# Routing of tokens with fewer VectorE operations, and the second item's expert and rows made first

## The chip, the cores and the metric

The kernel runs on one core of one Trainium2 chip. The metric is the device time of one execution in microseconds (us), the median of several runs. Engines are named as in the profile: PE is TensorE, DVE is VectorE, ACT is ScalarE, POOL is GpSimd, SP is SyncE, which issues most DMAs.

## What is computed

Three stages follow each other: attention, a mixture of experts with one expert for each token (MoE), and a dense layer (moe2).

```python
def attn(q, k, v):                       # 4 batches, 8 heads, 576 tokens, 64
    scores = where(causal window of 128, q @ k.T / 8 - slope[h] * |i - j|, -1e9)
    return softmax(scores) @ v           # 2304 tokens x 512

def moe(x, modality_id, w_gate, modality_bias, w1, w2):    # 8 experts
    logits = x @ w_gate + modality_bias[modality_id]
    e_idx = argmax(logits, axis=1)
    gate_w = softmax(logits)[arange(N), e_idx]
    out[tokens of e] = gate_w * (relu(x @ w1[e]) @ w2[e])  # w1 512x1024, w2 1024x512

def moe2(x, w_in, w_out):
    h = x @ w_in                         # 512 x 2048
    return (h * cos(h)) @ w_out
```

## The kernel before

**Attention** (0 to 186 us) runs over 36 units of four heads and 128 rows. The 2304 tokens are 18 blocks of 128. When a pair of blocks is done, its routing runs between the units: `logits(t)` gives `products` (the logits of 256 tokens as 16 rows: 8 experts as a high and a low part, ls), `choose` (ls transposed to tokens on partitions, parts and bias added, the largest found, ties broken by rev; the result is the one-hot oh, with a bf16 copy ohb) and `ranks(t)`: PE matmuls with the triangular matrix tri and the matrix ones count for each token how many earlier ones chose the same expert. cum is the running sum of oh over the pairs. DVE's `fold` (a multiplication and a reduction) picks the rank of the own expert, and the rank is split into rank // 128 and rank % 128 (pf). `one_hot` of the second part is ob.

**Items.** A work item is up to 256 tokens of one expert; nine items follow each other, each in eight steps (n = 0 to 71, and three more, since the second product lags by three). A step of item i has 12 matmuls `up` (xT with s1, the split of w1) and 12 matmuls `down` (hh with s2, the split of w2). Weights come in pieces of 512 KB on SP's queue (`load_w1`, `load_w2`) into r1 and r2, with two buffers each; the expert's number is read from the tile regs into a register of SP first (L230). ACT casts a piece into the high half of s, DVE subtracts it for the low half: both are needed for the product. POOL gathers an item's tokens with indirect DMAs (xg), PE transposes them and ACT and DVE split them into xT. Items 0 to 8 alternate between two tiles xT0 and xT1.

Item 0 takes its expert and rows from `early()`, which looks at the first blocks only and lets the item start before the routing is complete. All others need `late()`. Its pieces lie in the list `after`, and one is taken at each step: `sums` (for each expert the number of items, and their order), `slots` (each token's slot among the 26 blocks of 128 slots, one-hot in oa and multiplied by the row number), `table` (18 matmuls of oa with ob: the row behind each slot, idx), `experts` (the expert of each item, regs). Then `starts` and `gates`, `rows_of` and `dense`, which make the right-hand sides rhs and with 18 more matmuls the place and the gate of each token in the dense stage (tok_d, gate_d). 

**The order.** Every engine runs its instructions in the order in which they stand. Up to step 12 a scheduler sets this order by its own estimate of when things are ready; from step 12 to 66 (`InOrder`) it is the order in which the code is written. PE, DVE and ACT are each one queue. From step 10 on the conversion of the dense layer's weights (double precision words to f32, tiles mag, top, wi_a, lf) runs between the steps on DVE, ACT and POOL. The dense stage begins at about 376.

**Names.** s1_0 to s1_2 are the three split buffers of w1, s2_0 and s2_1 those of w2; numbers behind them are counted by the program. Instructions of the helpers carry the helper's line: L535 (attention and routing) and L1168 (items and dense) before, L549 and L1190 after.

Of the kernel before, what the change touches and what calls it, by code (L numbers as in the profile page):

```python
# [22 lines left out]
HALF_PI = 1.5707963267948966  # L23

# [5 lines left out]
def kernel(  # L30
# [162 lines left out]
    oh = rt.tile([128, T, NE], F32, name="oh")  # L193
    ohb = rt.tile([128, 2, NE], BF16, name="ohb")
    cum = rt.tile([128, NE], BF16, name="cum")
    iota = rt.tile([128, 128], F16, name="iota")
# [8 lines left out]
    regs = rt.tile([1, 2 * NL + 2], I32, name="regs")  # L205
    xTs = [rt.tile([128, 2, KD, SLOTS], F32R, name=f"xT{j}") for j in range(2)]
    xgs = [rt.tile([128, DM], F32, name=f"xg{j}") for j in range(2)]
    idx0 = rt.tile([128, 2], I32, name="idx0")
# [8 lines left out]
    def one_hot(out, n, at, count):  # L217
        V_.tensor_tensor(out, iota[:, 0:n].unsqueeze(1).to_broadcast([128, count, n]),
                         at.unsqueeze(2).to_broadcast([128, count, n]), op=ALU.is_equal)

    NF = FF // 128
    W1, HH = {}, {}
    E = {}
# [17 lines left out]
    def ranks(t):  # L241

        rp = E["rp"] = bank("L", [128, 3, NE])
        a, b = ohb[:, 0], ohb[:, 1]
# [6 lines left out]
        if t == 0:  # L251
            V_.tensor_tensor(cum, oh[:, 0], oh[:, 1], op=ALU.add)
# [12 lines left out]
    def early():  # L265
# [14 lines left out]
        def lacks():  # L280
# [5 lines left out]
            V_.scalar_tensor_tensor(cum[0:1], eo[0:1], short[0:1], cum[0:1], op0=ALU.mult, op1=ALU.add)  # L286
# [33 lines left out]
    def late():  # L320
# [12 lines left out]
        def sums():  # L333
            ci = rt.tile([128, 3, NE], I32, name="ci")
            V_.tensor_copy(ci[:, 2], E["rp"][:, 2])
            V_.tensor_scalar(ci[:, 0], ci[:, 2], 8, None, op0=ALU.logical_shift_right)
            V_.tensor_scalar(ci[:, 1], ci[:, 2], 255, None, op0=ALU.bitwise_and)
            V_.tensor_copy(K3[:, 0], ci[:, 0])
            V_.tensor_copy(rr, ci[:, 1])
# [14 lines left out]
            V_.tensor_scalar(A3[:, 0], pre[:, 0], 2.0, None, op0=ALU.mult)  # L354
            V_.tensor_scalar(A3[:, 1], K3[:, 0], 2.0, None, op0=ALU.mult)
            V_.tensor_tensor(endF, A3[:, 0], A3[:, 1], op=ALU.add)
            V_.tensor_tensor(A3[:, 2], pblk, endF, op=ALU.subtract)
            E["m9"] = m9

        def experts():  # L360
# [4 lines left out]
            nb = rt.tile([1, NE], F32, name="nb")  # L365
            V_.scalar_tensor_tensor(nb, K3[0:1, 1], 2.0, K3[0:1, 2], op0=ALU.mult, op1=ALU.add)
            V_.tensor_tensor(nb, nb, pblk[0:1], op=ALU.add)
            b = rt.tile(shp, F32, name="b_", tag="fold3")
            inF = rt.tile(shp, F32, name="inF")
            V_.tensor_tensor(inF, bl, rowp(A3[:, 0]), op=ALU.is_ge)  # L370
# [13 lines left out]
        def slots():  # L384
# [21 lines left out]
        def starts():  # L406
# [4 lines left out]
            n256 = rt.tile([128, 1], F32, name="n256")  # L411
            V_.tensor_scalar(n256, tot[:, 0:1], float(SLOTS), None, op0=ALU.mult)
            V_.tensor_scalar(ds, ds, n256, None, op0=ALU.add)
# [8 lines left out]
            V_.scalar_tensor_tensor(dq, A3[:, 2], 128.0, dq, op0=ALU.mult, op1=ALU.add)  # L422
# [15 lines left out]
        def rows_of():  # L438
# [3 lines left out]
            V_.scalar_tensor_tensor(dt, a3[:, 0], 128.0, dt, op0=ALU.mult, op1=ALU.add)  # L442
# [3 lines left out]
            di = rt.tile([128, T], I32, name="di")  # L446
            V_.tensor_copy(di, dt)
            dh = rt.tile([128, 2, T], I32, name="dh")
            V_.tensor_scalar(dh[:, 0], di, 7, None, op0=ALU.logical_shift_right)
# [1104 lines left out]
```

## Time and profile before

| | |
|---|---|
| median of 3 runs | 836.0 us (834.7 to 837.13) |
| the profiled execution | 837.98 us, of which the span is 836.3 |
| PE busy | 800.9 us (96%) |
| DVE busy | 615.7 us (74%) |
| ACT busy | 492.2 us (59%) |
| POOL busy | 198.3 us (24%) |

The profile is one execution. A row of a timeline gives the start, the busy time, the engine, the line, the operation with its tiles (result<-operands), shapes and count, and in brackets how long the engine was idle before it and who released it. Matmul times overlap in the pipeline, so the spacing of starts tells more about the cost of a small one than its duration does.

### The profile page before, as it was taken

The page shows a single profiled execution, that of the slowest core. Times are in us where ns is not written, and L with a number is a line of the kernel's source. Part 1 is how long each engine was busy: PE and PEld are TensorE (multiplying, and loading weights), DVE is VectorE, ACT ScalarE, POOL GpSimd, SP SyncE. Part 2 cuts the span into 40 slices and gives each one's busy share as a digit, 9 for nine tenths or more (in the row PEclk, how much of TensorE's full clock was granted, in tenths as well). Part 3 has the DMA queues.
Part 4 walks back from the last instruction along what each step waited for, and adds up shares of the span by engine and source line. Part 5 has one row for each costly group of instructions (what it writes and reads, how often), then busy time and mean ns, then how long its engine had stood idle before and what let it go on. Part 6 is the DMA issues. An engine that isn't in the chain of part 4 may idle for free. (4 is left out here: it accounts for less than half of the span.)

```text
span 836.3 us, 14761 instructions
## 1 busy us (share of the span) xinstructions
PE 800.9 (96%) x5278; PEld 704.9 (84%) x5278; DVE 615.7 (74%) x1472; ACT 492.2 (59%) x912; POOL 198.3 (24%) x256
## 2 busy tenths in 40 slices
PE   7999999998899999999999999999999999999996
PEld 5889888888889999999978788777888888888995
DVE  4767786768899999997749999886665555555562
ACT  6866766552565676665646676654544555444562
POOL 4755574411022132330001121112122002100100
PEclk9999999989899999999999999999999999999999
DMA  9664530452788888878633232402211001100000
GB/s 169 157 156 109 140 89 33 140 169 60 256 273 267 282 277 267 275 226 293 207 122 96 66 125 65 164 25 69 96 56 58 1 1 38 38 1 1 26 26 25
DMA packets 125134, 103.40 MB, mean 124 GB/s; under 512 B 61725, under 2 KB 105027, under 8 KB 125059
## 3 DMA queue, kind: packets, MB, share of 16 engines
q1 hardware_dynamic: 121043, 92.48, 37.0%
q0 software_dynamic: 2960, 9.70, 3.4%
q8 instruction: 42, 0.69, 0.3%
q10 hardware_dynamic: 1056, 0.26, 0.2%
q14 instruction: 33, 0.27, 0.1%
HBM read 85.90 MB, written 16.52 MB: 122 GB/s over the span
## 5 line engine op out<-in xcount | busy, mean ns | idle before, releaser
L1168 PE MATMUL bk<-hh,s 128*128 128x256 f32 x864 | 116.9, 283 | 5.2 <-DVE y L1168 4.5
L1168 PE MATMUL bk<-xT,s 128*128 128x256 f32 x816 | 111.8, 287 | 3.9 <-ACT s L1168 2.8
L1168 POOL TENSOR_TENSOR lf<-lf,mag 128x512 f32<-128x512 f32 x32 | 47.2, 1476 | 284.1 <-DVE mag L1168 258.9
L1168 PEld LDWEIGHTS bk<-hh,s 128*128 128x128 f32 x864 | 108.0, 189 | 6.7 <-DVE y L1168 5.3
L1168 PEld LDWEIGHTS bk<-xT,s 128*128 128x128 f32 x816 | 104.6, 195 | 4.5 <-ACT s L1168 3.0
L1168 PE MATMUL bk<-yT,wi_a 128*128 128x512 f32 (+1 forms) x480 | 104.1, 368 | 1.2 <-DVE yT L1168 0.8
L1168 PE MATMUL bk<-yT,wi_b 128*128 128x512 f32 (+1 forms) x480 | 104.8, 367 | 0.0
L1168 DVE TENSOR_TENSOR s<-r,s 128x1024 fp32r<-128x1024 f32 x70 | 92.8, 1327 | 12.3 <-ACT s L1168 10.2
L1168 ACT ACTIVATE r<-r 128x512 f32<-128x512 f32 (+1 forms) x80 | 47.2, 590 | 91.9 <-DVE r L1168 91.9
L1168 ACT CAST s<-r 128x1024 fp32r<-128x1024 f32 x70 | 73.3, 1050 | 45.1 <-DMA r<-in_moe_w_dram 30.5
L1168 PEld LDWEIGHTS bk<-yT,wi_a 128*128 128x128 f32 x480 | 83.7, 188 | 17.3 <-DVE yT L1168 1.1
L1168 PEld LDWEIGHTS bk<-yT,wi_b 128*128 128x128 f32 x480 | 84.4, 188 | 15.7
L1168 DVE TENSOR_TENSOR r<-bk,r 128x512 f32<-128x512 f32 (+1 forms) x80 | 50.9, 637 | 62.6 <-ACT r L1168 61.9
L1168 PE MATMUL bk<-wo_b,gg 128*128 128x512 f32 x384 | 94.8, 393 | 1.8 <-DVE po L1168 1.1
L1168 PE MATMUL bk<-wo_a,gg 128*128 128x512 f32 x384 | 92.7, 390 | 0.4 <-DVE gg L1168 0.3
L1168 PEld LDWEIGHTS bk<-wo_b,gg 128*128 128x128 f32 x384 | 71.0, 188 | 20.5 <-DVE gg L1168 2.4
L1168 PEld LDWEIGHTS bk<-wo_a,gg 128*128 128x128 f32 x384 | 71.9, 188 | 16.1 <-DVE gg L1168 1.2
L1168 DVE TENSOR_TENSOR gg<-r,gg 128x512 fp32r<-128x512 f32 x64 | 46.1, 720 | 34.7 <-ACT gg L1168 34.7
L535 PE MATMUL bk<-vt,pT 128*128 128x65 f32 x544 | 67.2, 277 | 0.2 <-POOL pT L535 0.2
L535 PEld LDWEIGHTS bk<-vt,pT 128*128 128x128 f32 x544 | 65.3, 196 | 1.8 <-issue 1.2
L1168 ACT CAST gg<-r 128x512 fp32r<-128x512 f32 x64 | 39.7, 620 | 40.9 <-DVE r L1168 40.0
L1168 DVE SCALAR_TENSOR_TENSOR r<-ki,bk 128x512 f32<-128x512 int32 (+1 forms) x80 | 50.4, 630 | 16.0 <-ACT ki L1168 15.3
(274 smaller groups left out, 1285.8 us busy)
## 6 DMA issues: line engine op xcount, KB each, us to landing
r<-in_moe_w_dram SPq DMA_DIRECT2D x72, 512.0 KB
y_dram<-y SPq DMA_DIRECT2D x19, 256.0 KB
rqk<-in_q_dram SPq DMA_DIRECT2D x32, 128.0 KB
vt<-in_v_dram SPq DMA_DIRECT2D x32, 128.0 KB
x_dram<-xt SPq DMA_DIRECT2D x16, 256.0 KB
raw<-in_moe_w_dram SPq DMA_DIRECT2D x8, 512.0 KB
yg<-y_dram SPq DMA_DIRECT2D x16, 256.0 KB
f64x<-in_moe_w_in_dram SPq DMA_DIRECT2D x8, 512.0 KB
```

The lines of the kernel that those rows point to most:

```text
L535: self.last = op(*args, **kwargs)
L1168: r = op(*args, **kwargs)
```

## The change

1. `choose`: the two transposes become two products with sel (16x8, the sum of two identity blocks), which add the high and the low part on PE. One add on DVE goes. oh is written once, in bf16; the copy ohb goes.
2. `ranks`: cum keeps the two blocks of a pair apart, [128, 2, 8]; one add on DVE instead of two, and one more matmul with ones in each of the three groups (8 matmuls become 11 from the second pair on). The rank is split by `by128`, which adds a large constant and subtracts it again: three operations on DVE instead of four. `rows_of` uses it too.
3. `sums` uses the same trick, and now also makes the expert of item 1 (at2, e1) into a register tile of its own, reg1, which `load_w1` reads for item 1.
4. `slots` makes only the two columns of item 1 (oa1); `rows1` turns them by 18 matmuls over 2 columns into idx1, from which item 1 is gathered. The whole oa (`all_slots`) and `table` follow behind that, in the second list.
5. The setup makes sel, a 128-wide iota with negative sign (parts128), and signs.

```diff
@@ by128 @@
+    def by128(out, src):
+        t = rt.tile([128, src.shape[1]], F32, name="to128", tag="to128_%d" % src.shape[1])
+        V_.tensor_scalar(t, src, -63.5, TO128, op0=ALU.add, op1=ALU.add)
+        V_.scalar_tensor_tensor(out[:, 1], t, TO128, src, op0=ALU.subtract, op1=ALU.subtract)
+        V_.tensor_scalar(out[:, 0], t, TO128, 1.0 / 128, op0=ALU.subtract, op1=ALU.mult)
@@ load_w1 @@
-            EV[i] = nc.sync.value_load(regs[0:1, rg:rg + 1], min_val=0, max_val=NE - 1)
+            EV[i] = nc.sync.value_load(reg1 if i == 1 else regs[0:1, rg:rg + 1], min_val=0, max_val=NE - 1)
@@ ranks @@
-        parts = [[(tri, a), (ones, cum)], [(tri, b), (ones, a), (ones, cum)], [(ones, a), (ones, b), (ones, cum)]]
+        parts = [[(tri, a)], [(tri, b), (ones, a)], [(ones, a), (ones, b)]]
...
-            ab = ab if t else ab[:-1]
+            ab = ab + [(ones, cum[:, 0]), (ones, cum[:, 1])] if t else ab
...
-            V_.tensor_tensor(cum, cum, oh[:, t], op=ALU.add)
-            V_.tensor_tensor(cum, cum, oh[:, t + 1], op=ALU.add)
-        ri = rt.tile([128, 2], I32, name="ri")
-        V_.tensor_copy(ri, rank[:, t:t + 2])
-        ph = rt.tile([128, 2, 2], I32, name="ph")
-        V_.tensor_scalar(ph[:, 0], ri, 7, None, op0=ALU.logical_shift_right)
-        V_.tensor_scalar(ph[:, 1], ri, 127, None, op0=ALU.bitwise_and)
-        V_.tensor_copy(pf[:, :, t:t + 2], ph)
+            V_.tensor_tensor(cum, cum, oh[:, t:t + 2], op=ALU.add)
+        by128(pf[:, :, t:t + 2], rank[:, t:t + 2])
@@ late: sums @@
+            V_.scalar_tensor_tensor(nb, K3[:, 1], 2.0, K3[:, 2], op0=ALU.mult, op1=ALU.add)
+            V_.tensor_tensor(nb, nb, pblk, op=ALU.add)
...
+            at2 = rt.tile([1, 4, NE], F32, name="at2", tag="fold3")
+            V_.scalar_tensor_tensor(at2, Q6[0:1, 2:6], 2.0, signed, op0=ALU.is_le, op1=ALU.mult)
+            e1 = rt.tile([1, 1], F32, name="e1_")
+            V_.tensor_reduce(e1, at2, op=ALU.add, axis=AX.XY)
+            V_.tensor_copy(reg1, e1)
@@ late: slots @@
-            one_hot(oa, NBLK, bh, T)
-            MK["oa"] = V_.tensor_tensor(oa, oa, row.unsqueeze(2).to_broadcast([128, T, NBLK]), op=ALU.mult)
+            oa1 = E["oa1"] = rt.tile([128, T, 2], F16, name="oa1")
+            one_hot(oa1, 2, bh, T, 2)
+            MK["oa"] = V_.tensor_tensor(oa1, oa1, row.unsqueeze(2).to_broadcast([128, T, 2]), op=ALU.mult)
+
+        def rows1():
+            tp = bank("T", [128, 2])
+            for t in range(T):
+                nc.tensor.matmul(tp, ob[:, t], E["oa1"][:, t], start=t == 0, stop=t == T - 1)
+            MK["idx1"] = V_.tensor_scalar(idx1, tp, float(NT // 2), None, op0=ALU.add)
+
+        def all_slots():
+            with tc.issue_after(MK["idx1"].ins):
+                one_hot(oa, NBLK, E["bh"], T)
+                V_.tensor_tensor(oa, oa, row.unsqueeze(2).to_broadcast([128, T, NBLK]), op=ALU.mult)
@@ late @@
-        return [sums, slots, table, behind_slots], [starts, gates, rows_of, dense]
+        return [sums, slots, rows1, behind_slots], [all_slots, table, starts, gates, rows_of, dense]
@@ choose @@
-                    nc.tensor.transpose(lt[:, j].rearrange("p a e -> p (a e)"), ls[:, 128 * j:128 * j + 128],
-                                        ident[:2 * NE, :2 * NE])
+                    nc.tensor.matmul(lt[:, j], ls[:, 128 * j:128 * j + 128], sel, start=True, stop=True)
...
-                nc.vector.tensor_tensor(lg, lt[:, :, 0], biasm[:, t:t + 2], op=ALU.add)
-                nc.vector.tensor_tensor(lg, lt[:, :, 1], lg, op=ALU.add)
+                nc.vector.tensor_tensor(lg, lt, biasm[:, t:t + 2], op=ALU.add)
```

**Where instructions move.** PE at the dense table of `dense`, before: xg_99 and xg_100 are the gathered rows of item 1 here, s_1_3517 and s_2_3518 are w1 buffers, s_1_3520 and s_0_3519 w2 buffers.

```order
L1168 MATMUL bk<-ident,xg_99 128x128 x4
L1168 MATMUL bk<-ident,xg_100 128x128 x4
L1168 MATMUL bk<-xT_98,s_1_3517 128x256 x24
L1168 MATMUL bk<-hh,s_1_3520 128x256 x12
L1168 MATMUL bk<-xT_98,s_2_3518 128x256 x12
L1168 MATMUL bk<-hh,s_1_3520 128x256 x12
L1168 MATMUL bk<-xT_98,s_2_3518 128x256 x4
L1168 LDWEIGHTS ob
L1168 MATMUL bk<-rhs,ob 128x54
```

The same place on PE in the changed kernel, from behind the transposes of item 1's rows to the first matmul on rhs (s_1_3521 and s_0_3520 are w2 buffers, the other s w1 buffers).

```order
L1190 MATMUL bk<-xT_100,s_1_3518 128x256
L1190 MATMUL bk<-hh,s_1_3521 128x256 x7
L1190 MATMUL bk<-xT_100,s_2_3519 128x256
L1190 MATMUL bk<-hh,s_1_3521 128x256 x14
L1190 MATMUL bk<-xT_100,s_1_3518 128x256 x23
L1190 MATMUL bk<-xT_100,s_2_3519 128x256 x11
L1190 MATMUL bk<-hh,s_1_3521 128x256 x2
L1190 MATMUL bk<-xT_100,s_2_3519 128x256 x12
L1190 MATMUL bk<-hh,s_0_3520 128x256 x12
L1190 MATMUL bk<-xT_100,s_0_3517 128x256 x12
L1190 LDWEIGHTS ob
L1190 MATMUL bk<-rhs,ob 128x54
```

The last `down` matmuls of item 0 (hh) came to stand behind the transposes, and more of item 1's products ahead of rhs. PE behind the 18 matmuls on rhs, before:

```order
L1168 MATMUL bk<-xT_98,s_2_3518 128x256 x8
L1168 MATMUL bk<-hh,s_0_3519 128x256 x4
L1168 MATMUL bk<-ident,gate_d 18x128
L1168 MATMUL bk<-hh,s_0_3519 128x256 x2
L1168 MATMUL bk<-xT_98,s_0_3516 128x256 x12
L1168 MATMUL bk<-hh,s_0_3519 128x256 x6
L1168 MATMUL bk<-ident,xg_99 128x128 x4
```

and PE behind them in the changed kernel:

```order
L1190 MATMUL bk<-ident,gate_d 18x128
L1190 MATMUL bk<-ident,xg_101 128x128 x4
L1190 MATMUL bk<-hh,s_0_3520 128x256 x12
L1190 MATMUL bk<-xT_100,s_0_3517 128x256 x12
L1190 MATMUL bk<-ident,xg_102 128x128 x4
```

The 32 matmuls that stood between rhs and the transposes of item 2 stand ahead of rhs now. DVE around rhs, before, with program numbers (r1 and r2 are loaded pieces):

```order
L1168 TENSOR_TENSOR s2_1_3520<-r2_3667,s2_1_3520 128x1024
L1168 TENSOR_TENSOR s1_2_3518<-r1_3717,s1_2_3518 128x1024
L535 TENSOR_TENSOR ob_90<-iota_87,pf_92 128x768 x2
L535 TENSOR_TENSOR d1_3858<-iota_87,pf_92 128x324
L1168 TENSOR_TENSOR s1_0_3516<-r1_3796,s1_0_3516 128x1024
L535 TENSOR_TENSOR rhs_3857<-d1_3858,val_88 128x18x18
L535 TENSOR_TENSOR rhs_3857<-d1_3858,gs_3541 128x18x18 x2
L1168 TENSOR_TENSOR s2_0_3519<-r2_3719,s2_0_3519 128x1024
```

DVE in the changed kernel, somewhat earlier in its queue: from item 1's tables to the gates.

```order
L1190 TENSOR_TENSOR s2_0_3520<-r2_3721,s2_0_3520 128x1024
L549 TENSOR_REDUCE ds_3539<-fold_3838 128x8
L1190 TENSOR_TENSOR s1_0_3517<-r1_3783,s1_0_3517 128x1024
L549 SCALAR_TENSOR_TENSOR ds_3539<-tot_3532,ds_3539 128x8
L1190 COPY y_4012<-bk_3675 128x256
L549 SCALAR_TENSOR_TENSOR dq_3842<-Q6_3533,ds_3539 128x8
L549 TENSOR_TENSOR fold_3845<-inP_3537,dq_3842 1x136
L549 TENSOR_REDUCE dr_3844<-fold_3845 1x17
L549 SCALAR_TENSOR_TENSOR dq_3842<-Q6_3533,dq_3842 128x8
L1190 SCALAR_TENSOR_TENSOR hh_3918<-bk_3865,hh_3918 128x512
L549 TENSOR_SCALAR dr_3844<-dr_3844,short_2896 1x17
L1190 TENSOR_TENSOR s1_1_3518<-r1_3902,s1_1_3518 128x1024
```

The splits s2_0 and s1_1 of item 1's second and third pieces, and y and hh, which stood behind rhs, stand ahead of the tables that lead to rhs; s2_1, s1_2 of the next pieces, a second y and a second hh follow, still ahead of rhs.

## Rows read from the trace of the kernel before

**Rows 1.** The page, part 1: busy time, share of the span, instructions.

```profile
PE 800.9 (96%) x5278; PEld 704.9 (84%) x5278; DVE 615.7 (74%) x1472; ACT 492.2 (59%) x912; POOL 198.3 (24%) x256
```

**Rows 2.** Windows: stretch, its length, busy time (instructions) of each engine, granted clock.

```profile
20.00:186.00 166.00, 157.03 (x1470) 141.57 (x1469) 118.84 (x602) 110.89 (x276) 88.60 (x144) 0.98 0.46 122
...
205.20:212.80 7.60, 2.12 (x12) 1.35 (x11) 5.81 (x25) 4.39 (x7) 1.89 (x2) 0.87 0.89 294
212.80:217.40 4.60, 4.60 (x21) 4.60 (x22) 4.50 (x9) 2.57 (x3) 0.00 (x0) 0.50 0.85 283
...
236.00:326.00 90.00, 84.77 (x705) 83.56 (x703) 85.92 (x117) 59.89 (x89) 26.74 (x18) 1.00 0.84 270
326.00:376.00 50.00, 50.00 (x422) 50.00 (x423) 49.23 (x67) 33.02 (x49) 14.69 (x10) 1.00 0.80 253
```

**Rows 3.** Timeline of PE, 205 to 213.

```profile
205.94 0.66 PE L1168 MATMUL bk<-ident,xg 128*128 128x128 f32 x4 [0.71 <-DMA xg<-x_dram,idx]
207.44 0.63 PE L1168 MATMUL bk<-ident,xg 128*128 128x128 f32 x4 [0.84 <-DMA xg<-x_dram,idx]
210.87 0.79 PE L1168 MATMUL bk<-xT,s 128*128 128x256 f32 x2 [2.80 <-ACT s L1168]
212.80 3.57 PE L1168 MATMUL bk<-xT,s 128*128 128x256 f32 x15 [1.13 <-DVE s L1168]
```

**Rows 4.** Timeline of DVE, SP's queue and ACT, 198 to 210.

```profile
198.59 0.60 DVE L535 TENSOR_REDUCE a<-fold 128x54 f32<-128x432 f32 x1
...
204.70 0.17 DVE L535 CAST regs<-ie 1x17 int32<-1x17 f32 x1
...
205.71 0.39 SPq L233 DMA_DIRECT2D r<-in_moe_w_dram  x1
...
209.77 1.04 ACT L1168 CAST s<-r 128x1024 fp32r<-128x1024 f32 x1 [0.85 <-DMA r<-in_moe_w_dram]
```

**Rows 5.** Timeline of PE at the first pair's transposes and a late rank.

```profile
39.24 0.29 PE L535 MATMUL bk<-ident,ls 16*128 16x16 f32 x2
39.46 0.55 PE L535 MATMUL bk<-ident,e 128*128 128x128 f32 x3
...
184.55 0.18 PE L535 MATMUL bk<-ohb,tri 128*128 128x8 bf16 x1 [0.27 <-DVE ohb L535]
...
185.32 1.08 PE L535 MATMUL bk<-xT,wg 128*16 128x256 f32 x8 [0.42 <-DVE fold L535]
```

**Rows 6.** Groups of PE's instructions by shape: busy us, mean ns, idle before.

```profile
L1168 PE MATMUL bk<-yT,wi_a 128*128 128x512 f32 x384 | 92.3, 390 | 1.2 <-DVE yT L1168 0.8 <-PEq L1370 0.5
...
L535 PE MATMUL bk<-oa,ob 128*128 128x2 f16 x12 | 0.5, 164 | 0.3 <-DVE lg L535 0.3
```

**Rows 7.** Waits of PE from 20 to 186: us in total, times, longest.

```profile
PE bk L535 <- DVE xt L535: 2.6, 4, 1.4
PE bk L535 <- DVE xT L535: 2.1, 3, 1.0
```

**Rows 8.** Windows of DVE alone, and its timeline, 200 to 222.

```profile
200.00:222.00 22.00, 19.13 (x59) 0.84 0.65 215
...
203.14 0.67 DVE L1168 SCALAR_TENSOR_TENSOR hh<-bk,hh 128x512 fp32r<-128x512 f32 x1
...
211.52 1.22 DVE L1168 TENSOR_TENSOR s<-r,s 128x1024 fp32r<-128x1024 f32 x1
...
221.06 0.90 DVE L535 TENSOR_TENSOR rhs<-d,gs 128x324 f16<-128x324 f16 x2
```

**Rows 9.** Timeline of PE at the dense table and item 2's transposes.

```profile
222.43 0.66 PE L1168 MATMUL bk<-rhs,ob 128*128 128x54 f16 x18
...
226.92 0.60 PE L1168 MATMUL bk<-ident,xg 128*128 128x128 f32 x4
...
230.21 0.60 PE L1168 MATMUL bk<-ident,xg 128*128 128x128 f32 x4
```

**Rows 10.** Waits of PE from 236 to 330: us in total, times, longest.

```profile
PE bk L1168 <- DVE y L1168: 4.5, 4, 1.8
```

More of the change, by code (lines that the diff above doesn't have):

```diff
@@ L23 @@
 HALF_PI = 1.5707963267948966
+TO128 = 1.5 * 2.0 ** 30
 F64_LOW = 2.0 ** -15
@@ L192 @@
     lgs = rt.tile([128, T, NE], F32, name="lgs")
[L193 to L196, printed above, removed]
+    oh = rt.tile([128, T, NE], BF16, name="oh")
+    cum = rt.tile([128, 2, NE], BF16, name="cum")
+    iota = rt.tile([128, 32], F16, name="iota")
+    parts128 = rt.tile([128, 128], F16, name="parts128")
     val = rt.tile([128, T], F16, name="val")
@@ L205 @@
     regs = rt.tile([1, 2 * NL + 2], I32, name="regs")
+    reg1 = rt.tile([1, 1], I32, name="reg1")
+    signed = rt.tile([1, 4, NE], F32, name="signed")
     xTs = [rt.tile([128, 2, KD, SLOTS], F32R, name=f"xT{j}") for j in range(2)]
     xgs = [rt.tile([128, DM], F32, name=f"xg{j}") for j in range(2)]
-    idx0 = rt.tile([128, 2], I32, name="idx0")
+    idx0, idx1 = (rt.tile([128, 2], I32, name=f"idx{j}") for j in range(2))
     idx = rt.tile([128, NBLK], I32, name="idx")
@@ L215, in fold, with one_hot @@
         V_.tensor_reduce(out, t, op=ALU.add, axis=AX.X)
-    def one_hot(out, n, at, count):
-        V_.tensor_tensor(out, iota[:, 0:n].unsqueeze(1).to_broadcast([128, count, n]),
+    def one_hot(out, n, at, count, first=0):
+        of = parts128 if n == 128 else iota[:, first:first + n]
+        V_.tensor_tensor(out, of.unsqueeze(1).to_broadcast([128, count, n]),
                          at.unsqueeze(2).to_broadcast([128, count, n]), op=ALU.is_equal)
+    def by128(out, src):
[3 more added lines that the diff above has]
+        V_.tensor_scalar(out[:, 0], t, TO128, 1.0 / 128, op0=ALU.subtract, op1=ALU.mult)
     NF = FF // 128
@@ L285, in lacks @@
             V_.tensor_scalar(short, short, 0.0, None, op0=ALU.max)
-            V_.scalar_tensor_tensor(cum[0:1], eo[0:1], short[0:1], cum[0:1], op0=ALU.mult, op1=ALU.add)
+            V_.scalar_tensor_tensor(cum[0:1, 0], eo[0:1], short[0:1], cum[0:1, 0], op0=ALU.mult, op1=ALU.add)
             one_hot(oa0, 2, pf[:, 0, 0:TE], TE)
@@ L333, in sums @@
         def sums():
[L334 to L339, printed above, removed]
+            c = E["rp"][:, 2]
+            to256 = TO128 * SLOTS / 128
+            V_.tensor_scalar(rr, c, 0.5 - SLOTS / 2, to256, op0=ALU.add, op1=ALU.add)
+            V_.tensor_scalar(K3[:, 0], rr, to256, 1.0 / SLOTS, op0=ALU.subtract, op1=ALU.mult)
+            V_.scalar_tensor_tensor(rr, K3[:, 0], -float(SLOTS), c, op0=ALU.mult, op1=ALU.add)
             V_.tensor_scalar(K3[:, 1], rr, 128.0, None, op0=ALU.is_gt)
@@ L364, in rowp @@
                 return ap[0:1].unsqueeze(1).to_broadcast(shp)
[L365 to L367 removed]
             b = rt.tile(shp, F32, name="b_", tag="fold3")
             inF = rt.tile(shp, F32, name="inF")
[L370 removed]
+            V_.tensor_tensor(inF, bl, rowp(A3[:, 2]), op=ALU.is_ge)
             V_.tensor_tensor(b, rowp(endF), bl, op=ALU.is_gt)
@@ L410, in starts @@
             fold(ds, g, rr.unsqueeze(1).to_broadcast(shp), shp, rt)
-            n256 = rt.tile([128, 1], F32, name="n256")
-            V_.tensor_scalar(n256, tot[:, 0:1], float(SLOTS), None, op0=ALU.mult)
-            V_.tensor_scalar(ds, ds, n256, None, op0=ALU.add)
+            V_.scalar_tensor_tensor(ds, tot[:, 0:1].to_broadcast([128, NE]), float(SLOTS), ds, op0=ALU.mult,
+                                    op1=ALU.add)
             dq = rt.tile([128, NE], F32, name="dq")
@@ L445, in rows_of @@
             V_.tensor_tensor(dt, dt, cond, op=ALU.subtract)
[L446 to L449, printed above, removed]
-            V_.tensor_scalar(dh[:, 1], di, 127, None, op0=ALU.bitwise_and)
-            V_.tensor_copy(pf, dh)
+            by128(pf, dt)
             for t0 in range(0, T, 6):
@@ L599 @@
         biasm = rt.tile([128, T, NE], F32, name="biasm")
+        sel = rt.tile([2 * NE, NE], F32, name="sel")
         rev = E["rev"] = rt.tile([128, NE], F32, name="rev")
@@ L619, in setup_route @@
         def setup_route():
+            nc.vector.tensor_tensor(sel, ident[:2 * NE, 0:NE], ident[:2 * NE, NE:2 * NE], op=ALU.add)
             nc.vector.tensor_copy(wg[:, :, 0], wr)
@@ L678, in setup_tables, with signs @@
                                     base=0, channel_multiplier=-1)
-            return turns + [middle]
+            def signs():
+                for j in range(4):
+                    nc.vector.tensor_scalar(signed[:, j], iota[0:1, 0:NE], -1.0 if j % 2 else 1.0, None, op0=ALU.mult)
+            return turns + [middle, signs]
         def window(s):
```

48 lines of the change are left out of this document (25 added, 23 removed).

## The prediction

> **What bounds the kernel now.** I read the page first: PE is busy 96% of the span [rows 1], so whatever PE waits for or runs at half speed ends up in the time. The view of windows then says where PE loses anything [rows 2]. In the attention part (20 to 186) it is busy 157.03 of 166 us, so work added to PE there lengthens the run nearly one for one. Between 205.2 and 212.8 it is busy 2.12 of 7.60 us: 5.5 us are lost. Then it runs from 212.8 to 217.4 without a gap, but at a granted clock of 0.50, which is 1.2 of 2.4 GHz: 4.60 us for work that full speed does in 2.3. From 236 to 326 it is idle for 5.2 us, while DVE is busy 85.92 of 90: there DVE sets the pace.
>
> The timeline shows what the 5.5 us are [rows 3]: PE transposes the gathered rows of item 1 (0.71 and 0.84 us of waiting for the gather), then waits 2.80 us for ACT and 1.13 for DVE to split the first weights of item 1. Those weights are late because of their address: the register tile is written by DVE at 204.70, SP issues the load at 205.71, and ACT starts the cast at 209.77, waiting for the DMA [rows 4]. The load thus takes 4.06 us from issue to use. This chain (register, load, cast) is what the change shortens.
>
> **The change, part by part.** Counts are from the order of the instructions, durations from the rows.
>
> *Ranks.* Eight of nine pairs get 3 more small matmuls: 24. The nearest row of that kind is the 128x2 table: 0.5 us for 12, or 0.04 each [rows 6]. 24 x 0.04 = 1.0 us on PE, nearly all in the attention part; I take +1.0, with 0 as the other end.
>
> *Logits through sel.* 18 transposes of ls become 18 products of plain f32 with sel. The transposes start 0.11 us apart: two of them lie between 39.24 and 39.46 [rows 5]. The trace has no product of plain f32 operands: in its f32 products the operands that a row shows being made are written as fp32r. From below the new product costs what the transpose does, 0.11. The dearest f32 product is the 128x512 one, 92.3 us for 384, 0.24 each [rows 6]; that is (0.24 - 0.11) x 18 = 2.3 us. The ends are near each other, so I take the middle, +1.2; the rival below asks whether it can be worse. The Trainium skill ("FP8 and Floating Point Precision", TensorE Precision Notes) has a rule that speaks against this edit: a true FP32 product takes four passes through the array, where the reduced form takes one. No run here shows it; it would put 5.9 us where I put 1.2.
>
> *Fewer DVE operations in the attention part.* One add and one copy of the one-hot go per pair, and in ranks the split of the rank and the sum into cum lose one each. PE waits for these results in the last pairs only: 0.27 us for ohb and 0.42 for fold [rows 5]. At best both go: -0.7, which I take (0 is the other end). Elsewhere DVE has idle time, and shorter work there earns nothing unless it is in front of something PE waits for (rival 2).
>
> *Item 1's expert and rows first.* The register of item 1 is now written right behind the sums, behind a fold of a3, and no longer behind oa, the expert tables and their reduction. Its CAST stands directly behind the reduction that makes a3, which ended at 198.59 + 0.60 = 199.19 [rows 4]; so it comes near 199.3 instead of 204.70, 5.4 us sooner, and the load with it. The rows of item 1 come from 18 matmuls over 2 columns instead of 26, and the whole table follows later: its two DVE operations and 18 matmuls are still there, so the small table is extra, 18 x 0.04 = 0.7 us of PE. With weights landing about 5 us earlier, and item 0's last 24 matmuls now standing behind item 1's transposes as filling, I expect the 5.5 us of idle time to go, and with it the 2.3 us at half clock, except for two shorter waits for the gather. Those were 0.71 and 0.84; I keep 1.1 for both.
>
> *What is late next.* The order shows it: the dense table's right-hand sides (rhs). On DVE they now stand behind four weight splits, two hh and two y that before came behind them. On PE the 18 matmuls on rhs now have 32 more matmuls ahead of them, all those that before filled the time behind them, and gate_d's transpose, item 2's transposes and the rest stand behind rhs. When does DVE finish rhs? Before at 221.06 + 0.90 = 221.96 [rows 8]. Moved in front: 4 x 1.22 for the splits, 2 x 0.67 for hh, and two y at no more than an hh each: 6.2 to 7.5, say 6.9. That gives 228.9 if DVE's idle time stays as it was. From 200 to 222 it is busy 19.13 of 22.00 [rows 8]; if earlier weights remove those 2.9 us, 226.0. The start of the routing's tail is 0.5 to 1 us earlier. The ends are 225 and 228.4; I take 226.5, since the earlier weights act on most of these waits.
>
> When does PE arrive there? It reached rhs at 222.43 [rows 9], without a wait. Take off 5.5 and 2.3, add 1.1 for the gather, 0.7 for the small table, and 32 matmuls. One of these costs 0.119: from 226.92 to 230.21 there are 24 and four transposes of 0.11 [rows 9]. 222.43 - 7.8 + 1.8 + 3.8 = 220.2. So PE, which is in order, waits 6.3 us at rhs (4.8 to 8.2), about as long as at the old place. Nothing covers it.
>
> *Where PE stands then.* rhs takes 0.66 [rows 9]. The transpose of gate_d follows directly (before, 12 matmuls lay between) and must wait for DVE's short operations on the result; I put 0.7 (0 to 1.4, the time of those 12). Item 2's first transposes then come at 226.5 + 0.66 + 0.7 = 227.9 instead of 226.92, 1.0 late. At the old stall the clock fell to 0.50 while PE was idle 5.5 of 7.6 us [rows 2]; the new idle stretch is longer and unbroken, so I charge most of the same price again, 2.0 of 2.3. PE is then 3.0 us late at the second transposes (230.21 before); the ends are 0.4 and 4.9.
>
> *What is given back.* From 236 to 326 PE waited 4.5 us for y on DVE [rows 10]. A late PE finds some of these results ready. But DVE in this stretch also waits for what PE makes, so it moves too, although one split of item 2 (1.22 us) is already done. I take half of the 3.0: +1.5 remains (ends -1.3, where DVE's lead counts in full, and 4.9). From 326 to 376 PE is busy 50.00 of 50 us [rows 2], so what is left there stays.
>
> Sum: +1.0 + 1.2 - 0.7 + 1.5 = +3.0 us. The profiled execution took 837.98 us (span 836.3 and 1.7 around it), 2.0 above the median of 836.0; on it the sum gives 841.0, on the median **839.0 us**.
>
> **Rivals.**
> 1. *The sel product runs in several passes.* If a plain f32 product with its weight load costs four of the 0.11 us of a transpose [rows 5], 18 of them add 0.33 x 18 = 5.9 us instead of 1.2, in the stage where PE is 95% busy: 839.0 + 4.7 = 843.7. For it: no f32 row in the trace is such a product. Against: the weights have 16 rows and the moving side 8 columns, so one might not see it. The rule of the Trainium skill named above would make it so.
> 2. *Faster: DVE frees PE in the attention part.* PE waits there 2.6 us for xt and 2.1 for xT on DVE, 7 waits in all [rows 7]. Operations of choose and ranks stand in DVE's queue between these. If the missing ones take half of that away (-2.4), sel costs nothing, and DVE's lead of 1.3 counts behind the new stall: 1.0 - 0.7 - 2.4 - 1.3 = -3.4, 832.6. It decides from the point where an xt or xT is queued directly behind a removed operation. Against: the waits are few and unevenly long, so chance places, and most operations are removed far from them.
> 3. *Nothing to measure.* The new wait at rhs is swallowed whole by DVE's stretch from 236, and sel is as cheap as the transpose: 1.0 - 0.7 + 0 to 1 = about 836.5. For it: 5.2 us of idle time there [rows 2] are more than the 3.0 that PE is late.
> 4. *The early register does not start the load early*, because something ahead on SP's queue holds it. Then the old stall stays and the new one is added: 843 or more. In the order nothing but loads of item 0 stands ahead, so this is unlikely.
>
> The Trainium skill ("TensorE: Matmul & The Clock Gate", Why this matters for your kernels) asks for no long idle gaps between bursts, since the array then falls back to its lower clock; the rows agree (0.50 behind the gap). By it the moved stall costs its half-clock stretch at the new place too; if the clock stayed up, the sum would be 1.0 lower.
>
> **How the numbers follow.** A measurement of this kernel tells changes of about 0.3% (2.5 us) from none, so faster means below 833.5, slower above 838.5. Forecast 0.41, by itself 837 to 841; rival 1 0.16; rival 3 0.25; rival 2 0.15; rival 4 0.03. Slower: 0.29 of the forecast's 0.41, and rivals 1 and 4, 0.48. Same: the other 0.12 and most of rival 3, 0.35. Faster: rival 2 and a little of rival 3, 0.17. The range reaches from 833.0, inside rival 2, to 844.0, which takes in the middle of rival 1; about 0.2 is left out.
>
> **What would show it.** Right: PE's waits at 205 to 213 shrink to about 1 us, and a wait of 5 to 8 us for DVE rhs stands before the 18 rhs matmuls near 220, with clock 0.50 behind it; PE waits for y from 236 to 326 are less than 5.2 in sum. The sel rows show their own spacing: 0.11 to 0.24, or over 0.4. Attention would end (186 before) 1 to 2 us later. Wrong: no wait at rhs (DVE got there in time, and I counted its queue wrongly); a load of item 1 that still lands near 209; attention that ends earlier, which makes it rival 2.

## The result, and the profile after

The changed kernel takes 840.42 us (median of 8 executions, 836.55 to 846.11) against 834.97 for the kernel before (8 executions): ratio 1.006, interval 1.003 to 1.0089. The same file in a later group of runs gave 839.0 against 833.99: 1.0049 [1.0024, 1.0073]. It is slower, by about 5 us. In the experiments below one execution of dense_later (4433.23 us) and one of mid_split (850.97 us) stand far above their fellows, and neither the medians nor the ratios given for these two contain them.

One thing is needed to read the two profiles. The profiled execution of after (836.55 us) is the quickest of its eight, and that of before (837.98) is slower than all of its eight. The granted clock in the attention part also differs from execution to execution (from 160 to 180 it is 0.83 in before and 1.00 in after). So the spans aren't compared, only stretches inside an execution.

The page, part 1, of the changed kernel:

```profile
PE 798.3 (96%) x5338; PEld 706.4 (85%) x5338; DVE 612.2 (73%) x1446; ACT 491.8 (59%) x912; POOL 198.7 (24%) x257
```

DVE has lost 26 instructions and 3.5 us of work, PE has gained 60 instructions [rows 1]. That tells nothing of the time. The windows do (stretch, length, busy time and instructions of PE, PEld, DVE, ACT, POOL, granted clock, DMA share, GB/s), here from the attention part on:

```profile
20.00:186.00 166.00, 160.27 (x1542) 145.79 (x1541) 120.16 (x590) 112.28 (x279) 87.89 (x144) 1.00 0.48 127
200.18:204.91 4.73, 0.00 (x2) 0.00 (x1) 2.17 (x5) 0.37 (x1) 0.00 (x0) 0.68 0.96 346
204.91:209.30 4.39, 4.39 (x23) 4.39 (x24) 2.16 (x3) 3.07 (x5) 1.89 (x2) 0.57 0.55 164
...
220.66:228.09 7.43, 0.00 (x2) 0.10 (x1) 7.20 (x17) 2.15 (x3) 0.00 (x0) 0.84 0.44 141
228.09:232.80 4.71, 4.15 (x34) 4.00 (x34) 1.41 (x5) 0.58 (x1) 0.00 (x0) 0.52 0.39 115
236.00:326.00 90.00, 87.61 (x739) 87.00 (x737) 86.29 (x120) 60.24 (x89) 26.95 (x18) 1.00 0.86 275
```

Where before had one idle stretch and one half-clock stretch behind it [rows 2], after has two of each: 4.73 us idle, then 4.39 us at 0.57, and 7.43 us idle, then 4.71 us at 0.52 (0.50 is 1.2 of 2.4 GHz). The work in the two slow stretches would have taken 1.9 and 2.0 us less at full clock (4.39 x 0.43, 4.15 x 0.48). From 236 to 326 PE is idle 2.4 us where it was 5.2.

What PE waits for, from its timeline (start, length, operation, idle time before and who ended it), answers rows 3 and rows 9:

```profile
204.91 1.12 PE L1190 MATMUL bk<-ident,xg 128*128 128x128 f32 x4 [4.73 <-DMA xg<-x_dram,idx]
...
228.09 0.97 PE L1190 MATMUL bk<-rhs,ob 128*128 128x54 f16 x18 [7.43 <-DVE rhs L549]
229.62 0.39 PE L1190 MATMUL bk<-ident,gate_d 128*18 128x128 f32 x1 [0.56 <-DVE gate_d L549]
229.80 1.06 PE L1190 MATMUL bk<-ident,xg 128*128 128x128 f32 x4
...
234.36 0.60 PE L1190 MATMUL bk<-ident,xg 128*128 128x128 f32 x4
```

The waits for ACT and DVE to split item 1's weights (2.80 and 1.13 us, rows 3) are gone: that part of the change does what it says. In their place stand 4.73 us for the gathered rows of item 1 and 7.43 + 0.56 us for rhs and gate_d. Why the gather is slow is in the timeline of SP's queue, POOL and DVE:

```profile
194.63 0.13 DVE L549 CAST reg<-e__3593 1x1 int32<-1x1 f32 x1
...
195.62 0.38 SPq L245 DMA_DIRECT2D r<-in_moe_w_dram  x1
...
196.70 0.16 DVE L549 TENSOR_SCALAR idx<-bk 128x2 int32<-128x2 f32 x1
...
197.13 1.37 POOL L1190 DMA_INDIRECT xg<-x_dram,idx  x1 [27.43 <-DVE nu L549]
197.45 0.37 SPq L250 DMA_DIRECT2D r<-in_moe_w_dram  x1
...
198.81 1.00 POOL L1190 DMA_INDIRECT xg<-x_dram,idx  x1 [0.30 <-issue]
```

SP issues the first weight load 1.5 us ahead of the first gather; the last of the four stands at 197.45. PE gets the rows at 204.91, 7.8 us after the issue of the gather. Before, the order was the other way round: first load at 205.71 [rows 4], rows used at 205.94 [rows 3], 3.4 us after the issue of the gather:

```profile
202.56 0.95 POOL L1168 DMA_INDIRECT xg<-x_dram,idx  x1 [31.81 <-DVE nu L535]
```

While PE waits in after, the DMA engines are 0.96 busy at 346 GB/s (the window from 200.18).

To compare stretches I take one anchor in every kernel: the first of the last ranks matmuls with tri (192.43 before, 187.97 after) and the first transposes of item 8. The same windows from one to the other, of before and then of after:

```profile
192.43:375.99 183.56, 172.58 (x1447) 170.22 (x1446) 172.75 (x296) 111.28 (x162) 45.30 (x32) 0.98 0.77 247
```

```profile
187.97:376.23 188.26, 172.68 (x1472) 171.32 (x1470) 171.18 (x296) 111.89 (x163) 45.69 (x32) 0.96 0.76 241
```

The stretch is 4.7 us longer (5.0 in the second profile of the changed kernel), and PE is busy in it for the same time, so idle time makes the difference. Some 0.5 us of it is work that only changed sides of the anchor: four more products of the items stand behind it now, at 0.119 us each. The loss of the change is thus found in this stretch. PE's lateness at item 2's second transposes is 8.6 us (from the anchor 46.39 us to 234.36; before 37.78 to 230.21); 3.9 of it are given back by item 8.

### The profile page after: what moved, and what is told of

It is laid out like the page before. It is cut to its first block, busy times and chain, and to the rows that moved or that the text cites. A ratio compares the mean times of both kernels' runs of the same rounds, so it can differ in the third digit from the quotient of the medians.

```text
span 834.8 us, 14852 instructions
## 1 busy us (share of the span) xinstructions
PE 798.3 (96%) x5338; PEld 706.4 (85%) x5338; DVE 612.2 (73%) x1446; ACT 491.8 (59%) x912; POOL 198.7 (24%) x257
## 5 line engine op out<-in xcount | busy, mean ns | idle before, releaser
L1190 PE MATMUL bk<-hh,s 128*128 128x256 f32 x864 | 119.4, 286 | 2.6 <-DVE y L1190 2.5
L1190 PEld LDWEIGHTS bk<-hh,s 128*128 128x128 f32 x864 | 110.2, 191 | 3.7 <-DVE y L1190 3.3
L1190 PE MATMUL bk<-xT,s 128*128 128x256 f32 x816 | 107.4, 280 | 0.0
L1190 PEld LDWEIGHTS bk<-xT,s 128*128 128x128 f32 x816 | 101.0, 188 | 0.0
L549 PEld LDWEIGHTS bk<-vt,pT 128*128 128x128 f32 x544 | 63.6, 192 | 1.8 <-issue 0.9
```

Of the source, the lines that this page charges most:

```text
L549: self.last = op(*args, **kwargs)
L1190: r = op(*args, **kwargs)
```

## The experiments

**Theory A**: the loss comes from the new waits behind the routing (gather, rhs, gate_d and the slow clock behind them), and the cheaper routing in attention is worth about nothing. **Rival B**: these waits are swallowed where DVE sets the pace, and PE's added work in attention (sel, ranks) makes the loss. All ratios are against the kernel before, run on the same chip.

**Both halves apart.** The label again is the changed kernel once more; item1_old has the new choose, ranks and by128, and item 1's expert and rows as before; item1_only has choose and ranks as before, and only the new order of item 1 (with by128).

```diff
@@ item1_old, against the changed kernel @@
-            EV[i] = nc.sync.value_load(reg1 if i == 1 else regs[0:1, rg:rg + 1], ...)
+            EV[i] = nc.sync.value_load(regs[0:1, rg:rg + 1], ...)
...
-        return [sums, slots, rows1, behind_slots], [all_slots, table, starts, gates, rows_of, dense]
+        return [sums, slots, table, behind_slots], [starts, gates, rows_of, dense]
@@ item1_only, against the changed kernel @@
-    oh = rt.tile([128, T, NE], BF16, name="oh")
-    cum = rt.tile([128, 2, NE], BF16, name="cum")
+    oh = rt.tile([128, T, NE], F32, name="oh")
+    ohb = rt.tile([128, 2, NE], BF16, name="ohb")
+    cum = rt.tile([128, NE], BF16, name="cum")
...
-                    nc.tensor.matmul(lt[:, j], ls[:, 128 * j:128 * j + 128], sel, start=True, stop=True)
+                    nc.tensor.transpose(lt[:, j].rearrange("p a e -> p (a e)"), ls[:, 128 * j:128 * j + 128],
+                                        ident[:2 * NE, :2 * NE])
...
```

> The changed kernel as it is, once more, for a second profile. Theory A (the time is lost at two places behind the routing: 4.7 us for item 1's gathered rows and 7.4 us for rhs, each with a half-clock stretch behind it): both waits stand in this profile too, within 1 us of the first, and the time is 838 to 842. Rival B (the executions differ, and the loss is in the attention part, by its clock or its added matmuls): the two waits vary by several us, and the attention part ends 3 us later or more where the time is long.

> The changed kernel with the expert and the rows of item 1 made as before (whole table first, register from the item table); all savings on DVE and the sums on PE stay. Theory A: the old stall is back (5 to 6 us of idle time and a half-clock stretch), the wait for rhs is gone, the gather is quick again; against the kernel before only the added PE time in attention is left (2.9 us for sel by the spacing in the changed kernel's profile, 0.6 for ranks), less what DVE gives: 835 to 838. If the PE additions cost nothing and the shorter DVE chains count: 831 to 834.

> The changed kernel with choose and ranks as before (transposes, f32 one-hot with a bf16 copy, 8 matmuls for the ranks): the new order of item 1 alone. Theory A: waits of 4 to 5 us for the gather and of 6 to 8 for rhs, an attention part as before; the time is that of the kernel before plus 1 to 4 us, 836 to 839. Rival C (all of the loss is the added PE time of attention): no slower than the kernel before, 832 to 835.5.

Measured: again 1.0049 [1.0024, 1.0073]; item1_old 834.91 us, 0.9995 [0.9968, 1.0022]; item1_only 837.06 us, 1.0036 [1.0012, 1.006]. From anchor to item 8: again 188.56, item1_old 181.88, item1_only 187.89 us. item1_only loses 3.0 us of the 4.1 that the changed kernel loses beside it, and item1_old loses none (-0.4 us, with an interval of 2.3 either way). So the loss goes with the order of item 1, in the main at least, and not with the arithmetic of the routing. PE's waits of item1_only from 186 to 236 (line, total, times, longest) are those of the changed kernel:

```profile
PE bk L1194 <- DVE rhs L551: 7.2, 1, 7.2
PE bk L1194 <- DMA xg<-x_dram,idx: 5.0, 1, 5.0
PE bk L1194 <- DVE gate_d L551: 0.6, 1, 0.6
```

**Is it rhs? First try: the dense table later.** Empty steps move dense, with its matmuls on rhs and gate_d's transpose, behind more of PE's work.

```diff
-        return [sums, slots, rows1, behind_slots], [all_slots, table, starts, gates, rows_of, dense]
+        return [sums, slots, rows1, behind_slots], [all_slots, table, starts, gates, rows_of] + [lambda: None] * 5 + [dense]
```

> The changed kernel with the dense table's 18 matmuls and what follows them taken five half-steps later from the list, so that some 70 more matmuls stand ahead of them on PE. Theory A: the wait for rhs falls from 7.4 to under 1 us and no half-clock stretch follows; the time falls by 4 to 8 us, to 833 to 836. Rival B (the DVE-bound stage from 236 on swallows whatever PE loses before it): the wait goes, but waits for y grow by as much, and the time stays within 1.5 us of the changed kernel's, 839 to 842.

Measured 838.8 us, 1.0053 [1.0027, 1.008]: nothing was won. It came out as neither theory has it: the wait at rhs is gone, but PE's timeline shows where it went:

```profile
231.64 0.66 PE L1190 MATMUL bk<-rhs,ob 128*128 128x54 f16 x18
240.03 0.37 PE L1190 MATMUL bk<-ident,gate_d 128*18 128x128 f32 x1 [7.74 <-DVE gate_d L549]
```

and DVE's timeline why:

```profile
232.95 0.68 DVE L1190 TENSOR_TENSOR xT<-bk,xT 128x512 fp32r<-128x512 f32 x1
233.54 1.22 DVE L1190 TENSOR_TENSOR s<-r,s 128x1024 fp32r<-128x1024 f32 x1
...
236.15 1.75 DVE L1190 TENSOR_TENSOR top<-top,wi_a 128x512 f32<-128x512 f32 x1
237.82 0.68 DVE L1190 SCALAR_TENSOR_TENSOR hh<-bk,hh 128x512 fp32r<-128x512 f32 x1
238.43 0.16 DVE L549 TENSOR_SCALAR tok_d<-bk 128x18 int32<-128x18 f32 x1
...
239.72 0.16 DVE L549 SCALAR_TENSOR_TENSOR gate_d<-gate_d,bk 128x18 f32<-128x18 f32 x1
```

The three short operations that turn the result of rhs into gate_d now stand behind item 2's hh, xT, s, top and hh on DVE, so the first comes 6.8 us and the last 8.1 us after the start of the rhs matmuls, and PE, in order, stops at gate_d's transpose instead. The wait moved by one dependent.

**Second try: the dense table later, and gate_d's transpose later still.** Two places are moved, not one.

```diff
-            gt = bank("T", [T, 128])
-            nc.tensor.transpose(gt, gate_d, ident)
+        def gates_out():
+            gt = bank("T", [T, 128])
+            nc.tensor.transpose(gt, gate_d, ident)
...
+        return [...], [all_slots, table, starts, gates, rows_of] + [lambda: None] * 4 + [dense] + [lambda: None] * 5 + [gates_out]
```

> The changed kernel with the 18 matmuls on rhs four half-steps later and the transpose of gate_d and its store five steps after that, so that neither has to wait for DVE. In the run before, the wait for rhs had only moved on to gate_d (7.7 us), which was the same DVE queue met one step later. Theory A: both waits go (7.5 and 0.6 us, and some 2 us of half clock): 832 to 836. Rival B (DVE is behind by as much, and PE meets it again at y): waits of PE from 236 to 326 grow from 2.5 to over 6 us, 837 to 841.

Measured 833.4 us, 0.9986 [0.9972, 1.0001]: level with the kernel before, and by the ratios (0.9986 against 1.0049 and 1.006) 5 to 6 us under the changed one. PE's waits from 186 to 236, and its windows from anchor to item 8:

```profile
PE bk L1192 <- DMA xg<-x_dram,idx: 4.8, 1, 4.8
PE bk L1192 <- DVE rhs L551: 2.7, 1, 2.7
```

```profile
193.11:375.01 181.90, 171.34 (x1472) 169.39 (x1471) 170.71 (x296) 110.94 (x163) 45.52 (x32) 0.99 0.77 250
```

rhs went from 7.43 to 2.7 us, gate_d from 0.56 to 0, the granted clock of the stretch from 0.96 to 0.99, and the stretch became 6.4 us shorter, though the gather still costs 4.8 us. So PE's waits at rhs and gate_d, with the slow clock behind, do reach the end of the run, and rival B, that they are swallowed, falls. Its other half, PE's added work in attention, fell with item1_old.

**Is it the gather?** reg_late gives the loads back their old address (the rows of item 1 are still made first, so the gather goes ahead of the loads); mid_split is dense_split with reg1 written somewhat later; mid_split_tr is that with the transposes of ls and two adds in choose, as before.

```diff
@@ reg_late @@
-            EV[i] = nc.sync.value_load(reg1 if i == 1 else regs[0:1, rg:rg + 1], ...)
+            EV[i] = nc.sync.value_load(regs[0:1, rg:rg + 1], ...)
@@ mid_split, against dense_split @@
-            V_.tensor_copy(reg1, e1)
+            E["e1"] = e1
...
+            with tc.issue_after(last.ins):
+                V_.tensor_copy(reg1, E["e1"])
```

> The changed kernel, with item 1's expert read from the item table as before the change; its rows still come first. One thing is moved: the four weight loads start 5 to 6 us later, behind the two gathers. Theory A: the gather, issued at 197 and 199, is no longer shared with 2 MB of weights and lands within 3.5 us; the wait of 4.7 us falls to 0 to 1 and a new one for the weights (1 to 3 us) appears; in the order rhs stands ahead of three weight splits again, so its wait falls under 3 us: 832 to 836. Rival (the gather is slow by itself, or its index comes late): the wait of 4.7 stays.

> The changed kernel with both: the register of item 1 written some 3 us later on DVE (behind the second gather's issue, but well ahead of the item table), and the dense part split as in the run above. Theory A: no wait over 1.5 us is left between 196 and 236, no half-clock stretch there; 9 to 12 us of PE's time are freed before 236, of which DVE's pace from 236 to 326 lets 3 to 7 through: 829 to 834. Rival B: all is swallowed there: 836 to 840.

> The run above, and the logits transposed again instead of multiplied by sel, with the second add on DVE: 0.16 us less for each of 18 on PE. If PE's added time in attention counts one for one, 2 to 3 us less than the run above; if DVE's added operation costs as much, no difference (within 1 us).

Measured: reg_late 833.17 us, 0.9983 [0.9962, 1.0005]; mid_split 832.71, 0.9987 [0.9967, 1.0006]; mid_split_tr 831.43, 0.9974 [0.996, 0.9989]. The timeline of reg_late:

```profile
198.55 1.38 POOL L1190 DMA_INDIRECT xg<-x_dram,idx  x1 [29.01 <-DVE nu L549]
...
202.34 0.66 PE L1190 MATMUL bk<-ident,xg 128*128 128x128 f32 x4 [0.76 <-DMA xg<-x_dram,idx]
202.94 0.38 SPq L245 DMA_DIRECT2D r<-in_moe_w_dram  x1
...
208.15 0.50 PE L1190 MATMUL bk<-xT,s 128*128 128x256 f32 x2 [2.29 <-ACT s L1190]
...
210.56 2.72 PE L1190 MATMUL bk<-xT,s 128*128 128x256 f32 x11 [1.92 <-DVE s L1190]
```

With the first load 4.4 us behind the gather, the rows are there 3.8 us after the issue; the old waits for the split weights are back (2.29 and 1.92), and with PE stopped there, none is left at rhs. In mid_split the first gather goes ahead of the loads and the second among them:

```profile
200.51 1.06 POOL L1194 DMA_INDIRECT xg<-x_dram,idx  x1 [0.30 <-issue]
200.84 0.38 SPq L245 DMA_DIRECT2D r<-in_moe_w_dram  x1
...
202.80 0.66 PE L1194 MATMUL bk<-ident,xg 128*128 128x128 f32 x4 [0.94 <-DMA xg<-x_dram,idx]
...
207.15 0.94 PE L1194 MATMUL bk<-ident,xg 128*128 128x128 f32 x4 [3.46 <-DMA xg<-x_dram,idx]
```

The first gather's rows are used 4.0 us after its issue (198.83), the second's 6.6 us. That the second stands behind the first does not explain it: in reg_late, with no load among them, the second takes 3.7 us (200.23 to 203.91). One kernel thus shows both cases: a gather issued ahead of the loads takes some 4 us, one that shares the engines with them 6.6 to 7.8. The Trainium skill ("Trainium Kernel Development and Optimization", Key Constraints) says that DMAs issued from different engines' queues run on the same 16 DMA engines and interleave; the runs agree, and give the price here.

What the gather's wait costs by itself in the time of the run, no run shows. It is 4.8 us in dense_split, 1.4 in reg_late and 4.4 in mid_split, and the three times lie within 0.7 us of each other. In reg_late the 4.2 us for the split weights stand in its place. In mid_split, which was expected to have no wait over 1.5 us, the second gather kept one of 3.46; its waits from 186 to 236 add up to 5.5 us where dense_split has 8.1. Yet its stretch from anchor to item 8 is 183.05 us, 1.2 longer: from 236 to 326 it waits 3.7 us for y on DVE where dense_split waits 2.5, at a clock of 0.98 where dense_split has 1.00. And dense_split is level with the kernel before although the gather's wait is still there in full.

**What sel costs.** old_tr is item1_old with the transposes of ls and two adds; split_tr is dense_split with them. item1_old_b and old_tr_b repeat a pair on one chip.

```diff
-                    nc.tensor.matmul(lt[:, j], ls[:, 128 * j:128 * j + 128], sel, start=True, stop=True)
+                    nc.tensor.transpose(lt[:, j].rearrange("p a e -> p (a e)"), ls[:, 128 * j:128 * j + 128],
+                                        ident[:2 * NE, :2 * NE])
...
-                nc.vector.tensor_tensor(lg, lt, biasm[:, t:t + 2], op=ALU.add)
+                nc.vector.tensor_tensor(lg, lt[:, :, 0], biasm[:, t:t + 2], op=ALU.add)
+                nc.vector.tensor_tensor(lg, lt[:, :, 1], lg, op=ALU.add)
```

> The changed kernel with the dense part split as in dense_split, and the logits transposed with the second add on DVE as before the change. Against dense_split (833.4) only sel is taken away. By PE's rows sel costs 0.27 us where a transpose costs 0.11, 18 times, 2.9 us; if that counts in the attention part: 830 to 832, and this kernel is faster than both. If the added operation on DVE costs as much as PE gains: 833 to 834.

> The kernel item1_old (item 1's expert and rows made as before the change), with the transposes and the second add back: what is left of the change are the bf16 one-hot, the ranks with 11 matmuls and the split by a large constant. If sel is the costly part of that half: 2 to 3 us less than item1_old, 832 to 833, and 0.1 to 0.3% under the kernel before. If nothing of that half matters: as item1_old, 834.5 to 835.5.

> item1_old once more, beside the next run on the same chip, since the two were timed on different calls and their difference (4 to 5 us) is larger than the 2.9 us that sel's rows on PE give. If sel costs what its rows say: 2 to 4 us more than the next run, about the time of the kernel before. If the first difference was scatter between calls: less than 1 us.

> old_tr once more: 2 to 4 us under the run before it, and 0.3 to 0.6% under the kernel before, if transposes for sel are what makes it faster; within 1 us of the run before it if not.

Measured: split_tr 833.2 us, 0.999 [0.9971, 1.0009]; old_tr 829.64, 0.9947 [0.9927, 0.9967]; item1_old_b 834.54, 0.9998 [0.997, 1.0026]; old_tr_b 830.26, 0.9956 [0.993, 0.9982]. In the changed kernel PE's timeline shows two products with sel from 39.16 to 39.70:

```profile
39.16 0.61 PE L549 MATMUL bk<-sel,ls 16*128 16x8 f32 x4
39.70 0.66 PE L549 MATMUL bk<-ident,e 128*128 128x128 f32 x4
```

and the group has 36 records for 18 products:

```profile
L549 PE MATMUL bk<-sel,ls 16*128 16x8 f32 x36 | 5.5, 256 | 0.0
```

Each product of plain f32 stands as two records and takes 0.27 us, where a transpose took 0.11 [rows 5]: 18 x 0.16 = 2.9 us. By time, taking sel out (with its add back on DVE) wins 4.3 us in old_tr_b against item1_old_b, 1.3 in mid_split_tr against mid_split, and 0.2 in split_tr against dense_split, where the ratios (0.999 and 0.9986) show nothing won. More than the expected 2 to 3 us came in the first pair, less in the others. 2.9 lies between these; each ratio has an interval of 1.2 to 2.3 us either way, so the price in time is open. **The best kernel is old_tr**: bf16 one-hot, two-block cum and by128, but the transposes of ls and the old order of item 1. It is under the kernel before in both of its runs, and by the ratios under the changed one.

## Why the prediction was right or wrong

The forecast was 839.0 us, +3.0, with slower as the likeliest sign. Slower is right and the time lies in the range; the size is +5. That the time is only 1.4 us off is in part luck: the forecast started from 836.0, the median of 3, and over 8 executions the kernel before takes 834.97. Point by point:

- *What bounds* (right). Idle time of PE made the difference: PE is busy for equal times in the stretch that grew (172.58 and 172.68).
- *Old stall* (right). The register is written at 194.63, the load issued at 195.62, the waits for the split weights are gone. Rival 4 is out.
- *Wait at rhs, gate_d, clock behind them* (right in place and size, the size by luck). Forecast 6.3, 0.7 and 2.0 us; the rows give 7.43, 0.56 and 2.0. DVE is busy 7.20 of the 7.43 us: it is its queue that is late. But counted from the start of the routing's tail both ends of the wait came 4.9 to 6 us later than forecast. DVE's stretch from the reduction that makes a3 to rhs, in before and then in after:

```profile
198.59:221.96 23.37, 17.62 (x135) 16.56 (x135) 20.36 (x63) 9.64 (x14) 3.88 (x4) 0.85 0.61 203
```

```profile
194.11:228.03 33.92, 21.61 (x192) 21.13 (x192) 26.55 (x72) 13.14 (x18) 4.26 (x4) 0.87 0.68 217
```

  It is 10.6 us longer. 6.2 of these are work, as counted (6.2 to 7.5); the other 4.4 are idle time of DVE, 7.4 us where it was 3.0 and where the forecast let it stay or go. The longest idle stretch is a wait for the transposed rows of the late gather:

```profile
206.68 0.69 DVE L1190 TENSOR_TENSOR xT<-bk,xT 128x512 fp32r<-128x512 f32 x1 [4.33 <-ACT xT L1190]
```

  PE comes to rhs 2.7 us later behind the same reduction (26.55 us, before 23.84), where 2.2 earlier was forecast. The gather made both late, and so the wait between them came out near the forecast.
- *Gather* (**the term that was wrong**). "I keep 1.1 for both" was taken from a trace in which the gather was issued 3.2 us ahead of the first load and met a DMA share of 0.36 until then (3.4 us to its use); in after the share is 0.99 from its issue to its use. The load moved forward as forecast (5.6 us against the anchor: 13.28 us behind it before, 7.65 now) and so passed the gather. It cost 4.73 us of idle time, and the slow stretch behind it 1.9 more. These are 5.5 us over the 1.1; PE's lateness at item 2's second transposes is 8.6 where 3.0 was forecast, 5.6 more. These are times on PE; what of them reaches the end of the run is argued, not isolated (see above).
- *Given back* (the share right, the size not). I took half of 3.0; it was 3.9 of 8.6, and y waits went from 4.5 us [rows 10] to 2.5:

```profile
PE bk L1190 <- DVE y L1190: 2.5, 2, 1.6
```

  What remains is 4.7 instead of 1.5. This is where the +3.0 became +5; with +1.5 in attention it would have been +6.2, so the next point must be nearer to nothing. Rival 3 counted on all of it being swallowed; dense_split, 6.4 us shorter in this stretch, speaks against it.
- *Attention* (net not resolved, terms off). Forecast: ranks +1.0, sel +1.2, DVE -0.7, together +1.5. item1_old, which has these edits and not the new order of item 1, came out at 0.9995, that is -0.4 us with an interval of 2.3 either way. Single profiles can't tell more: in the eight with the attention code of the changed kernel the anchor lies between 187.97 and 193.11, and in the one of before at 192.43. So the sign that was named for being wrong, attention that ends earlier, shows in the profiles of after (187.97 and 189.45) and decides nothing. Inside, sel was too cheap (2.9 by its rows: above the upper end of 0.24 each, far below rival 1's 0.44), ranks too dear (11 matmuls start within 0.29 us at the anchor where 8 took 0.22, some 0.6 us for the 24), and one gain was missed: the waits for xt, 2.6 us in all [rows 7], don't appear in the list of after. PE's idle time from 38 to the anchor fell from 7.2 to 3.9 us, in before and then in after:

```profile
38.00:192.43 154.43, 147.23 (x1373) 133.14 (x1370) 111.46 (x548) 97.32 (x236) 73.92 (x119) 0.98 0.44 119
```

```profile
38.00:187.97 149.97, 146.06 (x1407) 133.08 (x1406) 107.82 (x520) 96.67 (x236) 73.22 (x119) 1.00 0.46 123
```

The order on DVE tells of the longest of these waits. Before, a COPY_PREDICATED stood between den's reciprocal and xt:

```profile
108.37 0.17 DVE L535 RECIPROCAL den<-den 128x4 f32<-128x4 f32 x1
108.46 0.41 DVE L535 COPY_PREDICATED bk<-near,bk 128x256 f32<-128x256 uint8 x1
108.78 0.41 DVE L535 TENSOR_TENSOR xt<-bk,den 128x256 f32<-128x256 f32 x1
```

After, xt follows the reciprocal directly:

```profile
107.30 0.17 DVE L549 RECIPROCAL den<-den 128x4 f32<-128x4 f32 x1
107.50 0.42 DVE L549 TENSOR_TENSOR xt<-bk,den 128x256 f32<-128x256 f32 x1
107.84 0.75 DVE L549 COPY_PREDICATED bk<-near,bk 128x256 f32<-128x256 uint8 x2
```

So the effect of rival 2 came true on PE: 3.3 us less idle time, about what sel and ranks add by their rows (2.9 and 0.6). old_tr, without sel, is 0.44 to 0.53% under the kernel before, which fits; split_tr, with the same attention code, is only 0.1% under it, with its waits behind the routing, so the gain is not isolated. That the order on DVE is the cause is argued from these rows, not isolated either. item1_only, with choose and the matmuls of ranks as before and only by128 new in attention, has no xt wait, and its idle time from 38 to the anchor is 5.1 us; so the missing operations of choose can't be the whole cause.

## What to carry to other kernels

When a load is moved forward, look at what it passes, on every queue: the wait it removes is priced from the trace, but so must be the transfer that it now shares the DMA engines with. On engines that run in order, a wait that is moved comes out at the next dependent that stands too early; follow the chain to its end (here rhs, three short operations, gate_d) and move all of it. When operations go from an engine that is not the bound, compare the order around what the bound engine waits for, not only the sum of durations.

## What was not expected of the hardware

- A gather of rows whose issue comes 1.5 us behind that of the first weight load took 7.8 us to its use instead of 3.4, at a DMA share of 0.96 and 346 GB/s.
- A product of plain f32, 16x128 by 16x8, shows two PE records and takes 0.27 us, neither a transpose's 0.11 nor four times that.
- The clock in attention is not the same from one execution of a program to the next: in the window from 160 to 180 it was 1.00 in after and 0.91 in the second profile of the changed kernel (0.83 in before).
- The granted clock over the whole span fell with the change. Its mean was 0.985 to 0.986 in the timed executions of the changed kernel and 0.989 in those of before beside them; 0.0035 of 835 us are some 3 us of full clock, idle time in it included. The two profiles place this behind the anchor (0.96, and 0.95 in the second profile, against 0.98). So a part of the loss is clock, which a list of waits alone doesn't show.
